# In the loop of small slots the gather of w2 moves from the first part of a slot to the second part of the slot before

## The chip, the cores and the metric

The kernel runs on one core of a Trainium2 chip. The metric is device time of one execution in microseconds (us). The engines that matter are TensorE (PE, with its weight loads PEld), VectorE (DVE), ScalarE (ACT), GpSimd (POOL, which issues every indirect transfer) and SyncE (SP, which issues direct ones).

## The reference

Attention over the channels of four batches, and behind it a skip test and a mixture of eight experts, each token going to one expert:

```python
# attention: B, N, C = 4, 5056, 256
s = kn.transpose(0, 2, 1) @ qn / tau          # kn, qn: k and q over their column norms
a = softmax(s)
x = (v @ a).reshape(B * N, C)
# experts: E = 8, F = 1024
skip_score = x @ w_skip
do_compute = skip_score > 0
xc = x[do_compute]
e_idx = argmax(xc @ w_gate)                   # gate_w: its softmax probability
for e in range(E):
    mask = e_idx == e
    h = maximum(xc[mask] @ w1[e], 0.0)
    y[mask] = gate_w[mask, None] * (h @ w2[e])
out[do_compute] = xc + y                      # other tokens keep x
```

## The kernel before

A planner (`Plan`) orders attention, routing and the first expert slots by hand-set costs and due times. Routing writes a list of token numbers per expert. What is left after that is done in two dynamic loops: large slots of 1024 tokens (`Large.loop`, L431) and small slots of 128 tokens (`Small.loop`, L521). The change touches the small loop and the weights that are loaded ahead of both loops.

**A small slot** is 128 tokens of one expert. It needs the expert's `w1` and `w2` (256 x 1024 numbers of 4 bytes each, so 1.05 MB apiece), its list of tokens and its rows of x. POOL gathers each of these with an indirect transfer: `gather_w` (L221) for weights, `gather_x` (L209) for rows, and `scatter_x` (L214) writes the result rows back. Where a slot has the same expert as the slot two before it, its index is out of bounds on purpose (`wii`, L883) and the gather moves nothing. Buffers are doubled (U = 2): one loop iteration does two slots, u = 0 and u = 1, and o is the other of the two. The trace names the tiles as follows: `v1r` and `v2r` are the raw w1 and w2, `vc` and `vd` their row numbers, `yg` the rows of x, `yT` x transposed, `ph` and `po` the two products in PSUM, `yH` and `yL` the hidden values in two halves of precision, `v2s` the same split of w2, `yo` the result rows, `mP`, `mN`, `mc` and `ms` the token list as it moves from the slot after next to the slot whose rows are stored.

**A slot has two parts**, divided by `tc.stage_boundary()`; an iteration of two slots is four stages.

- First part: POOL gathers w2 for the next slot (`v2r[o]`), copies a list (`ms`, L528) and scatters the result rows of the slot before. PE makes `ph` (L539, 32 matmuls), ACT and DVE split w2 in four pieces (L501, L502) and turn `ph` into `yH` and `yL` (L542, L543).
- Second part: POOL moves the lists on (L549, L550), gathers w1 of the slot two later (`v1r[u]`) and x of the slot two later (`yg[u]`). PE makes `po` (L558, L559), with the transposes of the next slot's x between (L494); DVE adds `po` to x (`yo`, L564, L565).

**What orders it.** Each engine runs its own instructions in the written order, and reuse of semaphores ties the stages together: an engine may enter a stage only when every engine has signed off the stage before the previous one. With stages A(s), B(s) for the two parts of slot s, entering B(s+1) needs the sign-off of B(s) from all five engines. An engine signs off a stage during the next one, at the place that `behind(...)` marks (`previous_stage_wait`), and waits there until everything that it started in the stage being signed off is complete, transfers included. For POOL, `behind(G)` stands at the end of each part, so B(s) is signed off at the end of A(s+1).

**Ahead of the loops**, `load_rows` and `load_weights` (called by the planner's last tasks, L1122) fetch lists, rows and weights of the first two slots. The w2 of slot 1 is not among them: the first part of slot 0 gathers it.

Of the kernel before, what the change touches and what calls it, by code (L numbers as in the profile page):

```python
# [36 lines left out]
U = 2  # L37
# [106 lines left out]
def attn_moe(ctx: ExitStack, tc: tile.TileContext, q, k, vt, tau, w_skip, w_gate, w1, w2, out):  # L144
# [52 lines left out]
    def apart(i, group, reason):  # L197
        tc.declare_no_dep(i.ins, group=group, across_iterations=True, reason=reason)
        tc.add_to_no_dep_group(group, i.ins)
# [8 lines left out]
    def gather_x(to, ls, n=NTOK):  # L208
        apart(G.indirect_dma_start(  # L209
            out=to, out_offset=None, in_=out[0:n, :],  # L210
            in_offset=IndirectOffsetOnAxis(ap=ls[:, 0:1], axis=0), bounds_check=n - 1, oob_is_err=False), *ROWS)

    def scatter_x(ls, src):
        i = (G.indirect_dma_start(  # L214
            out=out, out_offset=IndirectOffsetOnAxis(ap=ls[:, 0:1], axis=0),
            in_=src, in_offset=None, bounds_check=NTOK - 1, oob_is_err=False))
        apart(i, *ROWS)
        return i

    def gather_w(src, to, rows):  # L220
        G.indirect_dma_start(  # L221
            out=to, out_offset=None, in_=src,
            in_offset=IndirectOffsetOnAxis(ap=rows, axis=0), bounds_check=E * P - 1, oob_is_err=False)

    def load_list(adi, i, to, NT, q=nc.sync):
        a = q.value_load(adi[0:1, ds(i, 1)], min_val=0, max_val=E * CAP)
        return q.dma_start(to, lst[ds(a, NT * P), :].rearrange("(p t) w -> p t w", t=NT))
# [4 lines left out]
    def behind(*engines):  # L232

        for e in engines:
            tc.previous_stage_wait(e.engine)
# [3 lines left out]
    class Large:  # L239
# [191 lines left out]
        def loop(self):  # L431
            with tc.For_i(0, self.n, 1, iteration_sync="staggered", hint_engines=(mybir.EngineType.PE,)) as i, tc.manual_schedule():  # L432
                V.tensor_copy(self.wc, self.wii[:, ds(i + 1, 1)])
                V.tensor_copy(self.wd, self.wii[:, ds(i + 1, 1)])
                self.put_last()
                self.take(1)
                self.gather(1)
                gather_w(w1, self.w1r, self.wc)
                behind(G, SP)
                self.first(True)  # L440
                tc.stage_boundary()
                load_list(self.adi, i + 1, self.lN[:, :8, :], 8)
                gather_w(w2, self.w2r, self.wd)
                for t in range(4):
                    self.second(0, t)
                    if t == 1:
                        behind(T, S, V, G, SP)
                        self.transposed(1)
                tc.stage_boundary()
                self.take(0)  # L450
                self.gather(0)
                behind(G, SP)
                self.first(False)
                tc.stage_boundary()
                for t in range(4):
                    if t < 2:
                        self.split_w1(2 * t)
                        self.split_w1(2 * t + 1)
                    self.second(1, t, t < 2)
                    if t == 1:  # L460
                        self.transposed(0)
                        behind(T, S, V, G, SP)
            self.put_last()

    class Small:
# [49 lines left out]
        def load_weights(self):  # L515
            for u in range(U):
                gather_w(w1, self.w1r[u], self.wc[u])
                if u < U - 1:
                    gather_w(w2, self.w2r[u], self.wd[u])

        def loop(self):  # L521
            with tc.For_i(0, self.n, U, iteration_sync="staggered") as i, tc.manual_schedule():  # L522
                for u in range(U):
                    o = (u + 1) % U
                    if u:
                        tc.stage_boundary()
                    gather_w(w2, self.w2r[o], self.wd[o])
                    G.tensor_copy(self.ls[o], self.lc[o])  # L528
                    scatter_x(self.ls[o][:, 0, :], self.ob[o])
                    behind(G)  # L530
                    for g in range(2):
                        for c in (0, 1, 2) if g == 0 else (3,):
                            self.split_w2(u, c)
                        ph = psum["h"].tile([P, 512], F32, name="ph")
                        for f in range(4):
                            po = ph[:, f * P : (f + 1) * P]
                            for kb in range(2):
                                fs = slice(kb * F + (4 * g + f) * P, kb * F + (4 * g + f + 1) * P)
                                T.matmul(po, self.w1r[u][:, fs], self.xT[u][:, kb, :], start=(kb == 0), stop=(kb == 1), skip_group_check=True)  # L539
                        fs = slice(4 * g, 4 * g + 4)  # L540
                        hH, hL = (h[:, fs, :].rearrange("p f t -> p (f t)") for h in (self.hH, self.hL))
                        S.activation(hH, ph, AF.Relu)  # L542
                        V.scalar_tensor_tensor(hL, ph, 0.0, hH, ALU.max, ALU.subtract)  # L543
                        if g == 0:
                            behind(T, S, V, SP)
                            V.tensor_copy(self.wc[u], self.wii[:, ds(i + (u + U), 1)])
                            V.tensor_copy(self.wd[u], self.wii[:, ds(i + (u + U), 1)])
                    tc.stage_boundary()
                    G.tensor_copy(self.lc[o], self.lN[o])  # L549
                    G.tensor_copy(self.lN[o], self.lP[o])  # L550
                    load_list(self.adi, i + (u + 2 * U + 1), self.lP[o], 1)
                    behind(SP)
                    gather_w(w1, self.w1r[u], self.wc[u])
                    gather_x(self.xg[u], self.lN[u][:, 0, :])
                    behind(G)
                    po = psum["o", u % 2].tile([P, 512], F32, name="po")
                    for f in range(NFB):
                        T.matmul(po, self.hH[:, f, :], self.w2s[:, f, :, :], start=(f == 0), stop=False, skip_group_check=True)  # L558
                        T.matmul(po[:, :C], self.hL[:, f, :], self.w2s[:, f, 0, :], start=False, stop=(f == NFB - 1), skip_group_check=True)  # L559
                        if f == 4:  # L560
                            self.transposed(o)
                            behind(T, S, V)
                    gate = self.lc[u][:, 0, 1:2].bitcast(F32)
                    V.scalar_tensor_tensor(self.ob[u], po[:, C:], gate, self.xr[u], ALU.mult, ALU.add)  # L564
                    V.scalar_tensor_tensor(self.ob[u], po[:, :C], gate, self.ob[u], ALU.mult, ALU.add)  # L565
            scatter_x(self.lc[U - 1][:, 0, :], self.ob[U - 1])
# [616 lines left out]
```

## Time and profile before

| | us |
|---|---|
| median of 3 runs (837.49 to 839.32) | 837.91 |
| the profiled execution | 838.44 |
| its span, first to last instruction | 836.7 |
| large loop, first to last matmul of its body | 466.64 to 745.70 |
| small loop, first to last matmul of its body | 750.07 to 831.03 |

The profiled execution takes 1.74 us more than its span. The small loop does ten slots. In a row of the timeline the columns are the start in us, the duration in us, engine, line, operation, output tile <- input tiles, shapes and count; in brackets the idle time of that engine just before, and what ended it. In a row of the stretches the columns are the stretch, its length, busy time and count of each engine, the granted clock of PE as a share of full speed, the mean busy share of the 16 DMA engines and what they moved in GB/s.

### The profile page before, as it was taken

Reading aid. Unit: us, or ns where it says so; the run is one execution under the profiler, and the core shown is the slowest. Engines: PE = TensorE matmul, PEld = TensorE weight load, DVE = VectorE, ACT = ScalarE, POOL = GpSimd, SP = SyncE. Lnnn points to the kernel's source line nnn. Section 1 sums busy time; section 2 is a strip of 40 time slices with the busy share of each in tenths; the row PEclk is TensorE's granted clock in tenths of the full one; section 3 lists DMA queues with packets and bytes.
Section 4 is the critical chain, followed back from the end, with each engine's and each line's share of the span. In section 5 each row is a group of like instructions: output and inputs, shape, how many; then the busy total and the mean of one; then the engine's idle time right before and its main releaser. Section 6 shows DMA issues by size and latency. Waiting matters only on the chain. (4 is left out here: it accounts for less than half of the span.)

```text
span 836.7 us, 13561 instructions
## 1 busy us (share of the span) xinstructions
PE 790.2 (94%) x4506; PEld 695.8 (83%) x4506; DVE 519.4 (62%) x1055; ACT 369.8 (44%) x583; POOL 430.5 (51%) x470
## 2 busy tenths in 40 slices
PE   6999999999979999999989699999999999988876
PEld 5888888998968988888878588888888888877876
DVE  4729758989958556455377646465555556455655
ACT  5449548867665425324212424233333333234543
POOL 3000377778657776767427752434343434426666
PEclk9999999999989999999999899999999999999999
DMA  8969869999364535123021521111111111107770
GB/s 322 400 242 361 346 189 297 397 305 340 103 225 135 165 83 191 56 71 114 26 61 53 197 58 38 51 39 56 44 48 46 44 50 44 31 28 254 258 268 4
DMA packets 58073, 126.35 MB, mean 151 GB/s; under 512 B 17556, under 2 KB 37804, under 8 KB 55472
## 3 DMA queue, kind: packets, MB, share of 16 engines
q1 hardware_dynamic: 17280, 62.99, 20.4%
q0 software_dynamic: 19520, 42.12, 15.3%
q10 hardware_dynamic: 21232, 20.72, 8.2%
q8 instruction: 22, 0.36, 0.2%
q14 instruction: 19, 0.16, 0.1%
HBM read 115.98 MB, written 32.59 MB: 178 GB/s over the span
## 5 line engine op out<-in xcount | busy, mean ns | idle before, releaser
L817 POOL DMA_INDIRECT lst<-pay,r_posi x160 | 177.0, 1106 | 164.4 <-DVE r_posi L814 93.1
L662 PE MATMUL s<-qt,kt 128*128 128x256 f32 x640 | 149.2, 384 | 7.7 <-DMA kt<-in_k 7.7
L214 POOL DMA_INDIRECT out<-xg,lc x78 | 81.7, 1047 | 130.0 <-DVE xg L345 112.9
L662 PEld LDWEIGHTS s<-qt,kt 128*128 128x128 f32 x640 | 119.0, 192 | 22.7 <-issue 8.1
L338 PE MATMUL po<-w2s,hH 128*128 128x512 f32 x384 | 136.4, 398 | 1.1 <-ACT hH L321 1.1
L321 ACT ACTIVATE hH<-ph 128x512 fp32r<-128x512 f32 x96 | 57.5, 599 | 127.3 <-PE ph L318 127.3
L339 PE MATMUL po<-w2s,hL 128*128 128x256 f32 x384 | 107.2, 279 | 0.0
L322 DVE SCALAR_TENSOR_TENSOR hL<-ph,hH 128x512 fp32r<-128x512 f32 x96 | 66.5, 692 | 54.1 <-ACT hH L321 52.8
L209 POOL DMA_INDIRECT xg<-out,lc x80 | 83.5, 1044 | 31.6 <-issue 19.5
L735 PE MATMUL px<-aH,vH 128*128 128x266 f32 x320 | 99.1, 310 | 0.3 <-ACT xo L742 0.3
L737 PE MATMUL px<-aH,vL 128*128 128x266 f32 x320 | 91.8, 287 | 0.0
L736 PE MATMUL px<-aL,vH 128*128 128x266 f32 x320 | 91.3, 285 | 0.0
L338 PEld LDWEIGHTS po<-w2s,hH 128*128 128x128 f32 x384 | 72.1, 188 | 18.0 <-ACT hH L321 1.5
L742 ACT COPY xo<-px 128x532 f32<-128x532 f32 x80 | 47.8, 603 | 73.2 <-PE px L737 73.0
L316 PE MATMUL ph<-xH,w1H 128*128 128x512 f32 x192 | 75.7, 394 | 3.4 <-PEq L432 3.4
L338 PE MATMUL px<-w2s,hH 128*128 128x512 f32 x224 | 78.7, 395 | 0.0
L317 PE MATMUL ph<-xL,w1H 128*128 128x512 f32 x192 | 75.4, 393 | 0.0
L318 PE MATMUL ph<-xH,w1L 128*128 128x512 f32 x192 | 75.4, 393 | 0.0
L339 PEld LDWEIGHTS po<-w2s,hL 128*128 128x128 f32 x384 | 72.3, 188 | 0.4
L344 DVE SCALAR_TENSOR_TENSOR xg<-po,lc,xg 128x256 f32<-128x256 f32 x48 | 23.2, 484 | 63.8 <-PE po L339 53.1
L339 PE MATMUL px<-w2s,hL 128*128 128x256 f32 x224 | 62.7, 280 | 0.0
L735 PEld LDWEIGHTS px<-aH,vH 128*128 128x128 f32 x320 | 60.4, 189 | 1.9 <-ACT xo L742 0.5
(205 smaller groups left out, 1591.9 us busy)
## 6 DMA issues: line engine op xcount, KB each, us to landing
vf<-in_vt SPq DMA_DIRECT2D x32, 640.0 KB, 5.3
qt<-in_q SPq DMA_DIRECT2D x31, 640.0 KB, 7.0
kt<-in_k SPq DMA_DIRECT2D x31, 640.0 KB, 7.5
out<-xo ACTq DMA_DIRECT2D x12, 1280.0 KB, 6.4
lst<-pay,r_posi POOLq DMA_INDIRECT x160
out<-xo ACTq DMA_DIRECT2D x4, 640.0 KB, 5.9
out<-xo ACTq DMA_DIRECT2D x4, 576.0 KB, 8.8
xg<-out,lc POOLq DMA_INDIRECT x80, 2.8
```

The source lines that it names most:

```text
L209: apart(G.indirect_dma_start(out=to, out_offset=None, in_=out[0:n, :], in_offset=IndirectOffsetOnAxis(ap=ls[:, 0:1], axis=0), bounds_check ...
L214: i = (G.indirect_dma_start(out=out, out_offset=IndirectOffsetOnAxis(ap=ls[:, 0:1], axis=0), in_=src, in_offset=None, bounds_check=NTOK - ...
L316: T.matmul(ph, self.w1H[:, fs], self.xH[:, kb, :], start=(kb == 0), stop=False)
L317: T.matmul(ph, self.w1H[:, fs], self.xL[:, kb, :], start=False, stop=False)
L318: T.matmul(ph, self.w1L[:, fs], self.xH[:, kb, :], start=False, stop=(kb == 1))
L338: T.matmul(po, self.hH[:, f, ts], self.w2s[:, f, :, :], start=(f == 0), stop=False, skip_group_check=True)
L339: T.matmul(po[:, :C], self.hL[:, f, ts], self.w2s[:, f, 0, :], start=False, stop=(f == NFB - 1), skip_group_check=True)
L662: T.matmul(sums[b][:, cb, :], kt[:, j % JH, cb * P : (cb + 1) * P], qt[:, j % JH, :], start=(ch == 0 and j == 0 and cb == 0), stop=(ch == ...
L735: T.matmul(px[:, i, :NA], vH[:, kb, js], aH[:, kb, :], start=(kb == 0), stop=False)
L736: T.matmul(px[:, i, :NA], vH[:, kb, js], aL[:, kb, :], start=False, stop=False)
L737: T.matmul(px[:, i, :NA], vL[:, kb, js], aH[:, kb, :], start=False, stop=(kb == 1))
L817: i = G.indirect_dma_start(out=lst, out_offset=IndirectOffsetOnAxis(ap=posi[:, t : t + 1], axis=0), in_=pay[:, t0 + t, :], in_offset=None, ...
```

## The change

The w2 gather leaves the first part of a slot and becomes the last of three gathers in the second part, for the slot two later. The w2 of slot 1 is loaded ahead of the loops.

```diff
         def load_weights(self):
             for u in range(U):
                 gather_w(w1, self.w1r[u], self.wc[u])
-                if u < U - 1:
-                    gather_w(w2, self.w2r[u], self.wd[u])
+                gather_w(w2, self.w2r[u], self.wd[u])
...
                     if u:
                         tc.stage_boundary()
-                    gather_w(w2, self.w2r[o], self.wd[o])
                     G.tensor_copy(self.ls[o], self.lc[o])
                     scatter_x(self.ls[o][:, 0, :], self.ob[o])
                     behind(G)
...
                     behind(SP)
                     gather_w(w1, self.w1r[u], self.wc[u])
                     gather_x(self.xg[u], self.lN[u][:, 0, :])
+                    gather_w(w2, self.w2r[u], self.wd[u])
                     behind(G)
```

On POOL, before, from the second part of slot u = 0 to the second part of u = 1. The rows of `L522 ISA` are the entries of stages; their list of waits also holds those of the sign-off that was written just ahead of them.

```order
L549 COPY mc_4874<-mN_4870 128x2
L550 COPY mN_4870<-mP_4872 128x2 [waits Pool_I-5467_stg1,DMAHW5_49]
L221 DMA v1r_4850<-in_w,vc_4865 128x2048 [waits DVE_I-5467_stg0,PE_I-5467_stg0,DMASW1_49]
L209 DMA yg_4854<-out,mN_4869 128x256 [waits DMAHW4_49]
L522 ISA [waits Pool_I-5467_stg0,PE_I-5012_stg0,DMASW0_I-5012_stg0,sem_stage_0_6612]
L221 DMA v2r_4852<-in_w,vd_4867 128x2048
L528 COPY ms_4875<-mc_4873 128x2
L214 DMA out<-yo_4863,ms_4875 20224x256 [waits Pool_I-5467_stg2,DVE_I-5467_stg1]
L522 ISA [waits Pool_I-5467_stg1,DMASW4_I-5012_stg0,DVE_I-5012_stg0,sem_stage_1_6613]
L549 COPY mc_4873<-mN_4869 128x2
```

And the same stretch of POOL in the changed kernel.

```order
L547 COPY mc_4874<-mN_4870 128x2
L548 COPY mN_4870<-mP_4872 128x2 [waits Pool_I-5470_stg1,DMAHW5_49]
L221 DMA v1r_4850<-in_w,vc_4865 128x2048 [waits DVE_I-5470_stg0,PE_I-5470_stg0,DMASW1_49]
L209 DMA yg_4854<-out,mN_4869 128x256 [waits DMAHW4_49]
L221 DMA v2r_4852<-in_w,vd_4867 128x2048 [waits DVE_I-5470_stg0,DMASW2_49]
L521 ISA [waits PE_I-5015_stg0,Pool_I-5470_stg0,sem_stage_0_6615]
L526 COPY ms_4875<-mc_4873 128x2
L214 DMA out<-yo_4863,ms_4875 20224x256 [waits Pool_I-5470_stg2,DVE_I-5470_stg1]
L521 ISA [waits Pool_I-5470_stg1,Pool_I-5015_stg0,DMASW4_I-5015_stg0,DVE_I-5015_stg0,sem_stage_1_6616]
L547 COPY mc_4873<-mN_4869 128x2
```

The order of the transfers on POOL stays w1, x, w2, scatter; the entry of a stage has moved from ahead of w2 to behind it. In the lists of waits, a name with the number of this loop (`I-5467`, `I-5470`) counts the instructions of an engine; the names with the other number are semaphores taken over from the large loop, one for each transfer that is signed off. At the second of the two entries, behind the scatter, there were two of them (w1, x) and now there are three (w1, x, w2). At the first entry there were two (w2, scatter) and now there is one (scatter).

On POOL ahead of the loops, before: the last gathers of weights, then the stores of the last rows done ahead (`xg_145`), the entry of the large loop (L432) and its first stores.

```order
L221 DMA w2r<-in_w,wd 128x2048
L221 DMA v1r_4850<-in_w,vc_4865 128x2048
L221 DMA v2r_4852<-in_w,vd_4867 128x2048
L221 DMA v1r_4851<-in_w,vc_4866 128x2048
L214 DMA out<-xg_145,lc_153 20224x256 x4
L432 ISA x3
```

And in the changed kernel.

```order
L221 DMA w2r<-in_w,wd 128x2048
L221 DMA v1r_4850<-in_w,vc_4865 128x2048
L221 DMA v2r_4852<-in_w,vd_4867 128x2048
L221 DMA v1r_4851<-in_w,vc_4866 128x2048
L221 DMA v2r_4853<-in_w,vd_4868 128x2048
L214 DMA out<-xg_145,lc_153 20224x256 x4
L432 ISA x3
```

One more gather of a whole w2 stands ahead of those stores and of the entry of the large loop.

## The prediction

> **What bounds the kernel now.** First the page's head, then the busy time of stretches, to see which part of the kernel has room.
>
> ```profile
> span 836.7 us, 13561 instructions
> 490.00:745.00 255.00, 255.00 (x1335) 218.08 (x1334) 146.40 (x254) 87.10 (x154) 101.87 (x109) 1.00 0.14 43
> 750.00:812.00 62.00, 53.34 (x382) 48.96 (x382) 36.44 (x77) 30.48 (x62) 38.39 (x52) 0.97 0.69 250
> 812.00:832.00 20.00, 17.17 (x118) 15.31 (x118) 11.71 (x24) 9.16 (x19) 13.81 (x19) 1.00 0.17 55
> ```
>
> The large loop (490 to 745) is PE without a gap: whatever delays its start is kept to the end. In the small loop PE is busy 53.34 of 62 us and no other engine more; the DMA share is 0.69 while weights still come and 0.17 in the last slots, which fetch none. So some wait there belongs to no engine's work. To find it, compare the start of `po` with that of the first `yL` of the same slot, in a slot with transfers and in one without.
>
> ```profile
> 794.41 0.68 DVE L543 SCALAR_TENSOR_TENSOR yL<-ph,yH 128x512 fp32r<-128x512 f32 x1
> 796.43 0.47 PE L558 MATMUL po<-v2s,yH 128*128 128x512 f32 x1 [1.30 <-DVE v2s L502]
> 819.68 0.68 DVE L543 SCALAR_TENSOR_TENSOR yL<-ph,yH 128x512 fp32r<-128x512 f32 x1
> 820.16 0.47 PE L558 MATMUL po<-v2s,yH 128*128 128x512 f32 x1
> 815.50:819.40 3.90, 3.77 (x32) 3.43 (x31) 2.53 (x5) 2.97 (x7) 2.72 (x3) 1.00 0.04 0
> ```
>
> In the slot whose gathers move nothing (share 0.04) `po` starts 0.48 us behind the first `yL`; the first four of its eight steps need no more. With transfers it starts 2.02 us behind. The bracket blames DVE, but DVE's work is the same in both. POOL's rows show what differs.
>
> ```profile
> 787.57 1.02 POOL L214 DMA_INDIRECT out<-yo,ms  x1 [2.34 <-DMA yg<-out,mN]
> 789.81 1.05 POOL L221 DMA_INDIRECT v1r<-in_w,vc  x1 [0.69 <-issue]
> 791.17 1.01 POOL L209 DMA_INDIRECT yg<-out,mN  x1 [0.31 <-issue]
> 792.49 1.00 POOL L221 DMA_INDIRECT v2r<-in_w,vd  x1 [0.30 <-issue]
> 796.39 0.19 POOL L549 COPY mc<-mN 128x2 int32<-128x2 int32 x1 [0.62 <-DMA yg<-out,mN]
> 797.56 1.05 POOL L221 DMA_INDIRECT v1r<-in_w,vc  x1 [0.66 <-issue]
> 806.61 1.05 POOL L221 DMA_INDIRECT v1r<-in_w,vc  x1 [0.69 <-issue]
> 814.20 1.05 POOL L221 DMA_INDIRECT v1r<-in_w,vc  x1 [0.66 <-issue]
> 790.00:791.50 1.50, 1.50 (x11) 1.36 (x10) 0.00 (x0) 0.95 (x3) 1.19 (x2) 1.00 0.05 1
> 791.50:797.75 6.25, 4.95 (x40) 4.65 (x39) 4.77 (x10) 2.98 (x6) 3.70 (x7) 1.00 0.94 359
> 797.75:798.25 0.50, 0.50 (x4) 0.41 (x4) 0.00 (x0) 0.00 (x0) 0.50 (x1) 1.00 0.30 79
> ```
>
> POOL's first copy of the second part (796.39) waited for the landing of x, gathered at 791.17, and PE's `po` starts at the same moment, 796.43: both pass the entry of the second part, which needs POOL's sign-off of the second part before, and that needs the landing of w1 and x. **The small loop is a ring through POOL's transfers**: entry, list copies, gathers of w1 and x, their landing, next entry. From one w1 gather to the next it takes 7.75, 9.05 and 7.59 us. The engines rest on it by 1.5 us (2.02 - 0.48).
>
> **The change part by part.**
>
> *What moves in time.* The w2 gather was issued 0.30 us behind the end of the x gather (792.49), although a stage's entry stood between: POOL already ran ahead. Behind x without the entry it starts at the same time. The order in the DMA queue, w1, x, w2, scatter, does not change either. So w2 comes no earlier to speak of, and the number of bytes in the loop falls by one w2, which goes ahead of the loops.
>
> *What moves in the signing off.* In the order of POOL the sign-off behind the scatter now covers three transfers, w2 among them. PE, DVE, ACT and SP stand at the entry of the second part behind it; `po`, then `yo`, then the next split of w2 queue up behind PE's wait. The ring is therefore closed by w2's landing, not by x's. The DMA engines are busy in one stretch from 791.50 to about 797.9 (share 0.94, then 0.30 of the next half us), and w2 is its end. From the w1 gather at 789.81 to there are 8.1 us. An estimated 0.3 us of notice takes it to 8.4; 0.7 us of entry and copies and the 1.17 us from the first copy to the next w1 gather (796.39 to 797.56) close the ring at 10.3 us. From the other side: the short turns of 7.75 and 7.59 us, and behind x one more w2 of 1.05 MB at the 410 GB/s of a full stretch (row of 767.30 below), which is 2.56 us, make 10.2 to 10.3. The long turn (9.05) had its scatter waiting for x, as at 787.57; in the change the scatter goes out while w2 is still on its way, so all turns come out alike. **I take 10.3**, between 10.0 (no notice) and 10.9 (the clock case among the rivals).
>
> ```profile
> 750.07 3.81 PE L539 MATMUL ph<-yT,v1r 128*128 128x128 f32 x32 [1.54 <-issue]
> 751.13 1.06 POOL L221 DMA_INDIRECT v2r<-in_w,vd  x1 [1.17 <-issue]
> 755.30 1.06 POOL L221 DMA_INDIRECT v1r<-in_w,vc  x1 [0.71 <-DVE yL L543]
> 753.64 0.48 PE L558 MATMUL po<-v2s,yH 128*128 128x512 f32 x1
> 812.99 0.47 PE L558 MATMUL po<-v2s,yH 128*128 128x512 f32 x1 [1.12 <-DVE v2s L502]
> 827.79 0.47 PE L558 MATMUL po<-v2s,yH 128*128 128x512 f32 x1 [0.74 <-DVE v2s L502]
> ```
>
> *How many turns.* The first w1 gather of the loop stands at 755.30 and the last that moves data at 806.61: seven, so seven entries wait for data, slots 1 to 7. Without a w2 gather ahead of it (1.06 us at 751.13 before) the first w1 gather comes sooner, but it must wait until PE has read the buffer, which ends with `ph` at 753.9 (750.07 + 3.81); with the 0.7 us of dispatch that its row shows that is 754.6. `po` starts 1.13 us ahead of a w1 gather (796.43, 797.56), so `po` of slot 1 comes at 754.6 + 10.3 - 1.15 = 763.75, and that of slot 7 six turns later, at 825.55. Before, it stands at 812.99: **+12.6 us**. Slots 8 and 9 have no data to wait for; the last step (820.16 to 827.79, 7.63 us) may shrink to the 7.17 us of the one before: -0.4. The extra gather behind the last x costs up to 1.3 us against the final scatter, and the scatter ahead of it, no longer behind a w2, gives as much back: 0.
>
> *Ahead of the loops.* One more gather of 1.05 MB on POOL and in the DMA queue, where both are full.
>
> ```profile
> 465.97 0.99 POOL L221 DMA_INDIRECT v1r<-in_w,vc  x1 [0.30 <-issue]
> 466.64 0.76 PE L316 MATMUL ph<-xH,w1H 128*128 128x512 f32 x1 [3.41 <-PEq L432]
> 474.49 1.05 POOL L214 DMA_INDIRECT out<-xg,lc  x1 [0.30 <-issue]
> 477.23 0.19 POOL L265 COPY lc<-lN 128x8 int32<-128x8 int32 x1 [1.68 <-DMA out<-xg,lc]
> 480.68 0.47 PE L338 MATMUL po<-w2s,hH 128*128 128x512 f32 x1 [1.15 <-ACT hH L321]
> 465.50:475.00 9.50, 8.36 (x29) 6.81 (x30) 4.38 (x9) 4.18 (x8) 7.37 (x8) 0.74 0.95 363
> 477.00:478.50 1.50, 1.50 (x9) 1.23 (x8) 0.69 (x1) 0.74 (x2) 0.66 (x2) 1.00 0.00 0
> ```
>
> PE enters the large loop at 466.64 behind a wait for all engines; POOL's dispatch of one more gather moves that by 0.6 to 1.3 us. The larger delay comes behind it: from 465.5 the DMA engines are full (0.95) with weights and then stores, and POOL's copy at 477.23 waits for the last store. One w2 more, 1.05 MB at 363 to 410 GB/s, moves it by 2.6 to 2.9 us, and with it POOL's sign-off, on which the second stage of the large loop, PE's `po` at 480.68, seems to wait: it starts 1.15 us late, and POOL's row gathers stand right ahead of it. The two delays overlap. Bounds: 0.6 (only the dispatch, if that `po` waits for something else) and 2.9, or some 1.7 more if PE's clock, which the first row of that window has at 0.74, recovers one window later. **I take 2.6**, by the copy at 477.23, the nearest row; nothing hides it, since PE has no gap from 490 on.
>
> *Sum.* 12.6 - 0.4 + 2.6 = 14.8 us on the profiled execution of 838.44, so 853.2. The median of the runs is 837.91, 0.5 less, so **853**.
>
> *A rule that speaks for the change.* The issue and the landing of w2 stand in the rows above: 792.49, and about 797.9. The Trainium skill, "DMA: Bandwidth & Descriptors", section "Rules for kernel authors", says to issue a transfer early, compute meanwhile, and wait on its semaphore late. By that rule a gather moved ahead of an entry should not lose and may win; here the rows show that it is issued 0.3 us sooner at most while its wait is put one part earlier, which is the second half of the rule turned round.
>
> **The rivals.**
>
> *1. Faster: the entry waits for POOL's work, not for the landing.* Then a w2 gather less in the first part (1.00 us and 0.30 us ahead of it) brings the sign-off forward.
>
> ```profile
> L558 PE MATMUL po<-v2s,yH 128*128 128x512 f32 x80 | 32.1, 431 | 9.9 <-DVE v2s L502 5.4 <-DVE yL L543 4.5
> ```
>
> PE waits 9.9 us in all ahead of `po` in this loop, in seven places; 1.3 us off each is at most 9.1, and with 2.6 us ahead of the loops the time would be 838.4 - 9.1 + 2.6 = 832. It decides if POOL's first part is longer than the landing of x. Against it: at 820.16 POOL had done the same instructions and PE did not wait, and the copy at 796.39 names the landing of x. Chance 0.05. By the rule of the Trainium skill quoted above the time would come out here.
>
> *2. Only the load ahead of the loops counts*: w2 lands before x's landing is acted on, or is not waited for. Then 838.4 + 2.6 = 841. For it: w2 is hidden today. Against it: the third transfer in the sign-off. Chance 0.06.
>
> *3. The clock falls.* From `po` of slot 0 (753.64) to that of slot 7 (812.99) a slot takes 8.48 us, and PE is busy 53.34 of 62 us: 7.3 us of work a slot. In a turn of 10.3 us it rests 3 us.
>
> ```profile
> 767.30:770.70 3.40, 1.40 (x13) 1.20 (x11) 3.06 (x7) 1.41 (x3) 1.10 (x2) 1.00 1.01 410
> 770.80:774.10 3.30, 3.20 (x10) 2.75 (x11) 0.00 (x0) 0.00 (x0) 2.17 (x5) 0.50 0.13 43
> 770.90 0.77 PE L558 MATMUL po<-v2s,yH 128*128 128x512 f32 x1 [2.20 <-DVE yL L543]
> 784.40:787.80 3.40, 1.55 (x14) 1.36 (x13) 3.31 (x8) 1.56 (x3) 1.05 (x3) 1.00 1.03 410
> ```
>
> Before, PE was busy 1.40 us of a 3.4 us stretch and the granted clock fell to 0.50 for the next 3.3 us; with 1.55 us it did not fall. With longer rests it may fall in every turn. A stretch of 3.3 us at half speed costs a slot some 1.65 us of PE, on top of the 7.17 us that a slot takes without the ring (812.99 to 820.16): 8.8, still under 10.3, so hidden; with two such stretches 10.5. Then turns of 10.9 us give 4.2 us more in seven, some 857. The Trainium skill, "TensorE: Matmul & The Clock Gate", section "Why this matters for your kernels", warns of rests over about 3 us between bursts of matmuls; the trace agrees that rests cost clock, though here 2.20 us were enough once. Chance 0.14.
>
> **How the numbers follow.** The forecast (about 848 to 856) has 0.72, the clock case 0.14, the load alone 0.06, faster 0.05, others 0.03 (0.01 faster, 0.02 no change). The low end takes turns of 10.0 us (-2.1) and 0.6 us ahead of the loops (-2): 849, and 1.5 us of doubt on the first turn; the high end turns of 10.9 us and 1.7 us of clock at 480: 859. The range is 847 to 859.5. A measurement can tell about 0.2% (1.7 us) from no change: slower by more than that has 0.92 (the first three), within 0.02, faster 0.06.
>
> **What would show it.** Right: w1 gathers of POOL some 10.3 us apart in all seven turns; POOL's first copy of a second part released by `v2r`'s landing; DMA engines at rest for 3 us or more of each turn; PE waiting about 3 us ahead of `po`; the large loop's first `po` some 2.6 us later. Wrong: turns still of 7.7 and 9 us, or `po` starting within 0.5 us of `yL` in slots with transfers.

## The result, and the profile after

The changed kernel takes 857.66 us (median of 6 runs, 855.49 to 860.07) against 838.55 us (median of 6 runs of the kernel before, 837.49 to 839.93). The ratio is 1.0225, 95% interval 1.0207 to 1.0244: **slower by 2.2%**, 19 us. The profiled execution took 856.37 us, 17.93 more than that of before.

The head of the page after, and the busy time of three stretches (columns as before: PE, PEld, DVE, ACT, POOL, granted clock, DMA share, GB/s).

```profile
span 854.8 us, 13564 instructions
490.00:745.00 255.00, 255.00 (x1336) 218.06 (x1335) 145.85 (x253) 86.98 (x154) 102.59 (x110) 1.00 0.14 44
752.50:830.00 77.50, 57.23 (x395) 52.63 (x393) 37.43 (x78) 31.20 (x62) 38.54 (x54) 0.93 0.54 201
784.40:787.80 3.40, 1.36 (x13) 1.17 (x11) 2.72 (x7) 1.31 (x3) 1.24 (x1) 1.00 0.98 395
789.00:792.40 3.40, 3.22 (x10) 2.77 (x11) 0.00 (x0) 0.00 (x0) 2.19 (x4) 0.50 0.14 20
```

The large loop is as full as before. In the small loop PE is busy 0.74 of the time (before 0.86), the DMA engines 0.54 (before 0.69), and the clock is down to half in some stretches. POOL's timeline shows what a turn is made of. The rows are those of one turn, and the first and the eighth w1 gather of the loop, which enclose seven turns.

```profile
759.78 1.06 POOL L221 DMA_INDIRECT v1r<-in_w,vc  x1 [0.45 <-DVE v2s L502]
769.87 1.05 POOL L221 DMA_INDIRECT v1r<-in_w,vc  x1 [0.66 <-issue]
771.23 1.00 POOL L209 DMA_INDIRECT yg<-out,mN  x1 [0.31 <-issue]
772.53 1.00 POOL L221 DMA_INDIRECT v2r<-in_w,vd  x1 [0.30 <-issue]
778.91 0.18 POOL L547 COPY mc<-mN 128x2 int32<-128x2 int32 x1 [1.05 <-DMA v2r<-in_w,vd]
780.09 1.05 POOL L221 DMA_INDIRECT v1r<-in_w,vc  x1 [0.69 <-issue]
831.06 1.05 POOL L221 DMA_INDIRECT v1r<-in_w,vc  x1 [0.66 <-issue]
yg<-out,mN POOLq DMA_INDIRECT x7, 4.5
v2r<-in_w,vd POOLq DMA_INDIRECT x7, 5.6
768.72 0.77 PE L557 MATMUL po<-v2s,yH 128*128 128x512 f32 x1 [3.15 <-issue]
778.93 0.47 PE L557 MATMUL po<-v2s,yH 128*128 128x512 f32 x1 [1.90 <-DVE yL L541]
```

The eighth and ninth rows, from the list of transfers, give the median time from issue to landing, 4.5 us for x and 5.6 for w2: for the w2 of 772.53 that is 778.13. At 778.91 POOL's first copy of the next second part is released by just this transfer, and PE's `po` follows at 778.93. So the sign-off is closed by w2, where it was closed by x. A turn here is 2.66 us from the w1 gather to the w2 gather, 5.6 to the landing, 0.78 to the entry, and 1.18 over the two copies to the next w1 gather, together 10.22. The seven turns have a mean of (831.06 - 759.78) / 7 = **10.18 us; before it was (814.20 - 755.30) / 7 = 8.41**.

Where 18.1 us of span went, stage by stage, each from rows of the two timelines: the warming matmuls between the loops start at 752.23 instead of 746.95, +5.28; from there to the first w1 gather 7.55 instead of 8.35, -0.80; the seven turns 71.28 instead of 58.90, **+12.38**; from the eighth gather to the end 23.74 instead of 22.50, +1.24. The sum is 18.10, and the spans differ by 854.8 - 836.7 = 18.1.

The 5.28 ahead of the small loop come from the first stages of the large one, of which these are the rows after (the last is a stretch):

```profile
463.27 0.66 PE L282 MATMUL pt<-ident,xg 128*128 128x128 f32 x4 [1.63 <-DVE xL L286]
468.18 1.00 POOL L221 DMA_INDIRECT v2r<-in_w,vd  x1 [0.31 <-issue]
480.81 0.19 POOL L265 COPY lc<-lN 128x8 int32<-128x8 int32 x1 [3.49 <-DMA out<-xg,lc]
484.26 0.47 PE L338 MATMUL po<-w2s,hH 128*128 128x512 f32 x1 [3.35 <-issue]
485.20:488.60 3.40, 3.40 (x13) 2.84 (x12) 0.00 (x0) 0.00 (x0) 2.48 (x4) 0.50 0.35 88
```

The added gather (468.18) makes the last store late, the copy that waits for it stands at 480.81 instead of 477.23 (+3.58), and PE's `po` at 484.26 instead of 480.68 (+3.58 too). Of this 0.91 was there ahead of the gather, in the transposes of the first row (463.27, before 462.36), so 2.67 belongs to it. PE has then rested 3.35 us instead of 1.15, and the next 3.4 us go at half clock: half of that stretch, 1.7 us, is lost on top. Together that is 3.58 + 1.7 = 5.28, of which 4.4 (2.67 + 1.7) are the change's. No run explains the other 0.91.

### The profile page after: what moved, and what is told of

Read it like the earlier page. It is cut to its first block, busy times and chain, and to the rows that moved or that the text cites. A ratio compares the mean times of both kernels' runs of the same rounds, so it can differ in the third digit from the quotient of the medians.

```text
span 854.8 us, 13564 instructions
## 1 busy us (share of the span) xinstructions
PE 796.6 (93%) x4506; PEld 701.6 (82%) x4506; DVE 519.3 (61%) x1055; ACT 369.4 (43%) x583; POOL 428.1 (50%) x471
```

## The experiments

Theory: the longer turn is the landing of w2, which the sign-off of the second part now includes; and the load ahead of the loops costs some microseconds of its own. Rivals: the load ahead is all; POOL's own work is what got longer; the clock. For each kernel the mean of the seven turns between the first and the eighth w1 gather of the small loop is given beside the ratio, since it doesn't depend on what comes ahead.

Each ratio is to runs of the kernel before that were made beside it. For the first four experiments (load ahead, load between, emptied, halved) these took 839.89 us (median of 19 runs, 836.88 to 842.80). For the others they took 890.94 to 895.59 us, and everything ahead of the small loop took some 55 us longer; why isn't known. Single runs there spread over 9 to 25 us, so the intervals of the ratios are wide, and only turns and ratios are read. Neither the kernel before nor the changed one was profiled beside those, so their turns are compared with the 8.41 and 10.18 us of the profiles above.

### Only the load ahead of the loops

In the kernel before:

```diff
-                if u < U - 1:
-                    gather_w(w2, self.w2r[u], self.wd[u])
+                gather_w(w2, self.w2r[u], self.wd[u])
```

> The kernel before, and w2 of slot 1 is gathered ahead of the loops too; the first part of slot 0 gathers it once more, so the small loop stays as it was. Theory: the whole w2 put ahead of the large loop's first stores delays the rows of its first slot and brings the half-clock stretch one window later; 2.6 to 4.4 us, so 841 to 843 us, with gathers of w1 in the small loop 7.6 to 9.1 us apart as before. Rival (the load is hidden behind attention, and all of the loss is in the small loop): 838 to 839 us.

It took 842.53 us, ratio 1.0028 (1.0012 to 1.0044), so +2.4 us with 1.0 to 3.7 as bounds. Rows of its timeline: the large loop's first `po`, and the warming matmuls.

```profile
486.14 0.50 PE L338 MATMUL po<-w2s,hH 128*128 128x512 f32 x1 [3.67 <-issue]
754.06 1.58 PE L1128 MATMUL m<-ones 128*128 128x128 f32 x12 [1.25 <-PEq L432]
```

PE rests 3.67 us ahead of that `po`, about as in the changed kernel (3.35); in the kernel before it rests 1.15. The turns are 8.26 us, (820.05 - 762.21) / 7. So the load ahead costs time, and it is not all of the cost: the ratio of the change is 1.0225.

### The load between the loops

In the changed kernel:

```diff
     def load_weights(self):
         for u in range(U):
             gather_w(w1, self.w1r[u], self.wc[u])
-            gather_w(w2, self.w2r[u], self.wd[u])
+            if u < U - 1:
+                gather_w(w2, self.w2r[u], self.wd[u])
...
         keep_warm(6)
+        gather_w(w2, smalls[0].w2r[1], smalls[0].wd[1])
         smalls[0].loop()
```

> The changed kernel, but the w2 of slot 1 is gathered between the two loops instead of ahead of both. Theory (the load ahead costs 2.6 to 4.4 us, the small loop's longer turns cost the rest): 853 to 855 us, the large loop's first matmul back at about 466.6 us and the turns of the small loop still 10.2 us; 855 to 858 us if the entry of the small loop waits for the transfer to land (about 5 us, partly beside the last matmuls of the large loop). Rival (the load ahead is all of the cost): 838 to 841 us.

It took 855.30 us, ratio 1.0181 (1.0157 to 1.0205).

```profile
480.57 0.47 PE L338 MATMUL po<-w2s,hH 128*128 128x512 f32 x1 [1.41 <-ACT hH L321]
746.83 1.57 PE L1129 MATMUL m<-ones 128*128 128x128 f32 x12 [1.26 <-PEq L432]
756.65 0.18 POOL L548 COPY mc<-mN 128x2 int32<-128x2 int32 x1 [3.49 <-issue]
757.89 1.05 POOL L221 DMA_INDIRECT v1r<-in_w,vc  x1 [0.73 <-issue]
```

The large loop is back to the times of before (480.57 against 480.68, 746.83 against 746.95), with no half clock there. But the first second part now waits 3.49 us (third row), so the first w1 gather comes 11.06 us behind the warming matmuls instead of 7.55: 3.5 us of what is won ahead are paid here. The turns stay long, 10.47 us, one of them of 12.16 us (798.57 to 810.73), whose cause was not traced. Both parts of the theory stand. The load ahead costs 2.4 us by the medians of the kernel that has it alone, 4.4 by the profile of the changed kernel; this kernel doesn't narrow that down.

### The gather in the loop emptied, and halved

In the changed kernel, with a bound of one row (a fourth argument of `gather_w`), so that every row number but one is out of bounds; w2 of all but the first two slots is left out:

```diff
-                    gather_w(w2, self.w2r[u], self.wd[u])
+                    gather_w(w2, self.w2r[u], self.wd[u], 1)
```

And with 64 of the 128 rows, the other half of w2 being left out:

```diff
-                    gather_w(w2, self.w2r[u], self.wd[u])
+                    gather_w(w2, self.w2r[u][0:64], self.wd[u][0:64])
```

> The changed kernel, but the gathers of w2 inside the small loop drop every row but one, so they move next to nothing; w2 of all but the first two slots is left out, and the instructions stay where they are. Theory (a turn ends when the last byte of w2 has landed): the turn falls from 10.2 to 7.5 to 8.5 us, as long as w1 and x alone take or shorter; seven turns make 12 to 19 us less, 839 to 846 us. Rival (the length comes from POOL's own work, a third transfer to issue ahead of the sign-off): turns stay at 9.5 to 10.2 us and the time at 853 to 858 us.

> The changed kernel, but the gathers of w2 inside the small loop fetch 64 of the 128 rows, half the bytes; the other half of w2 of the later slots is left out. Theory (the turn ends with the last byte of w2): about half of the way from the empty gather to the whole one, turns of 8.8 to 9.4 us and 847 to 852 us. Rival (a fixed price for a third transfer in the sign-off, whatever its size): turns of 10.0 to 10.3 us and 856 to 858 us.

The emptied one took 841.99 us, ratio 1.0036 (1.0016 to 1.0055); the halved one 861.43 us, ratio 1.0239 (1.0215 to 1.0262). From the lists of transfers and from POOL's timeline, first the emptied, then the halved:

```profile
v2r<-in_w,vd POOLq DMA_INDIRECT x7, 3.4
759.63 1.06 POOL L221 DMA_INDIRECT v1r<-in_w,vc  x1 [0.45 <-DVE v2s L502]
774.00 1.30 POOL L214 DMA_INDIRECT out<-yo,ms  x1 [2.68 <-DMA v2r<-in_w,vd]
818.44 1.05 POOL L221 DMA_INDIRECT v1r<-in_w,vc  x1 [0.65 <-issue]
```

```profile
v2r<-in_w,vd POOLq DMA_INDIRECT x6, 6.2
764.47 1.06 POOL L221 DMA_INDIRECT v1r<-in_w,vc  x1 [0.45 <-DVE v2s L502]
838.98 1.05 POOL L221 DMA_INDIRECT v1r<-in_w,vc  x1 [0.65 <-issue]
781.00:782.90 1.90, 1.33 (x12) 1.14 (x11) 1.90 (x7) 1.28 (x3) 0.40 (x1) 1.00 0.65 134
```

Emptied, the same instructions at the same places give turns of 8.40 us, as before the change: the price is the transfer, not POOL's work. What is left of the ratio is about that of the load ahead alone (1.0028).

Halved, my expectation missed: the turns are not shorter but longer, 10.64 us. The list of transfers says why: 64 rows into 64 partitions land 6.2 us behind the issue, later than 128 rows (5.6). In the last row, the end of such a transfer, the DMA engines are busy at a share of 0.65 and move 134 GB/s, where a stretch of whole transfers has 395 at 0.98. The Trainium skill, "DMA: Bandwidth & Descriptors", section "Rules for kernel authors", asks for 128 partitions and at least 1 MiB per transfer for the most bandwidth; this transfer has neither, and the trace agrees, without telling the two apart. So bytes were a bad dose, but the landing is a good one: by the sum above (2.66 + landing + 0.78 + 1.18) landings of 5.6 and 6.2 us give 10.2 and 10.8, measured 10.18 and 10.64. With the 3.4 of the emptied gather the sum gives 8.0. Four of the seven turns there take 7.83 to 7.99 us and agree. The other three take 9.04 to 9.05: in them the scatter waits 2.7 us for a landing before it is issued (row of 774.00), as the scatter at 787.57 does in the kernel before, whose turns alternate in the same way.

### The clock

In the changed kernel, 16 more matmuls behind `ph`, so that PE doesn't rest so long:

```diff
+                    wm = psum["h"].tile([P, 512], F32, name="ph")
+                    for _ in range(16):
+                        T.matmul(wm[:, :P], self.w1r[u][:, :P], self.xT[u][:, 0, :], start=True, stop=True, skip_group_check=True)
                     tc.stage_boundary()
```

> The changed kernel, with 16 more matmuls of 128x128 (about 1.9 us at full clock) behind the ph of each small slot, into a PSUM tile that nobody reads, so that PE rests 1.3 us instead of 3.2 ahead of an entry. Theory (the half-clock stretches in every second slot are hidden beside the wait for w2): granted clock back to 1.0 in the small loop, turns still 10.0 to 10.3 us, 855 to 858 us. Rival (the half clock is part of the loss, 1.65 us in four or five slots): 849 to 852 us.

It took 920.90 us, ratio 1.0221 (1.0135 to 1.0307). A stretch of 60 us of its small loop, and its first and eighth w1 gather:

```profile
810.00:870.00 60.00, 58.62 (x477) 56.54 (x477) 27.94 (x58) 23.23 (x46) 28.07 (x39) 1.00 0.51 186
820.66 1.06 POOL L221 DMA_INDIRECT v1r<-in_w,vc  x1 [4.02 <-PE ph L548]
892.80 1.05 POOL L221 DMA_INDIRECT v1r<-in_w,vc  x1 [0.65 <-issue]
```

The clock is 1.00 and the turns are still 10.31 us. In the changed kernel it is 0.50 to 0.51 for 3.4 us behind every second entry (those of 768.72, 789.18, 809.61 and 829.97) and 1.00 behind the entries between. Up to the last of them, which no turn follows, that half clock was hidden beside the wait for w2.

### The order of the three gathers

In the changed kernel w2 first:

```diff
+                    gather_w(w2, self.w2r[u], self.wd[u])
                     gather_w(w1, self.w1r[u], self.wc[u])
                     gather_x(self.xg[u], self.lN[u][:, 0, :])
-                    gather_w(w2, self.w2r[u], self.wd[u])
```

> The changed kernel, with the three gathers of the second part in the order w2, w1, x instead of w1, x, w2. Theory (the turn ends when the last of the 2.2 MB has landed, and these move one behind the other at the rate of the DMA engines): turns of 10.0 to 10.4 us, 855 to 859 us. Rival (each transfer has its own latency from its issue, 4.5 us for x and 5.6 for weights, so that x last would end 1.1 us sooner): turns of 9.0 to 9.3 us, 848 to 851 us.

It took 918.63 us, ratio 1.0229 (1.0142 to 1.0316). The turns are 11.45 us, (893.94 - 813.78) / 7: longer, where I expected no change and the rival a gain. An entry of its second part, and the list of transfers:

```profile
845.53 0.18 POOL L547 COPY mc<-mN 128x2 int32<-128x2 int32 x1 [4.05 <-DMA v1r<-in_w,vc]
yg<-out,mN POOLq DMA_INDIRECT x4, 6.6
```

The bracket names w1 now, and x lands 6.6 us behind its issue instead of 4.5. That it doesn't keep its 4.5 us refutes the rival: the transfers stand one behind the other. Why the three together take 9.3 us (2.67 + 6.6) from the first issue instead of 8.3 stays open. The trace counts a landing in sixteen steps: of those of the x issued at 838.19, fourteen are there by 843.80, and the last two come at 844.82 and 844.85.

### What stands between entry and issue

The two list copies stand between the entry and the w1 gather. They were put behind the gathers, in the kernel before as shown, and in the changed one in the same way with the gather of w2 as the third:

```diff
+                    gather_w(w1, self.w1r[u], self.wc[u])
+                    gather_x(self.xg[u], self.lN[u][:, 0, :])
                     G.tensor_copy(self.lc[o], self.lN[o])
                     G.tensor_copy(self.lN[o], self.lP[o])
...
-                    gather_w(w1, self.w1r[u], self.wc[u])
-                    gather_x(self.xg[u], self.lN[u][:, 0, :])
```

> The kernel before, with the gathers of w1 and x issued ahead of the two list copies in the second part instead of behind them and behind the list load. Theory (a turn is entry, issue, landing, sign-off, next entry, and the copies stand between entry and issue): the first gather is issued about 0.7 us sooner after the entry, so turns of 7.6 to 7.8 us on average instead of 8.4, seven of them 4 to 6 us less, 833 to 836 us. Rival (turns are bound by the work of PE, ACT and DVE in a slot, and the copies hide beside it): 837.5 to 840 us.

> The changed kernel, with its three gathers issued ahead of the two list copies instead of behind them. In the kernel before, the same edit was worth nothing. Theory (in the changed kernel the ring runs through the landing, with room on POOL, so what stands between entry and issue counts in full): turns 0.4 to 1.0 us shorter, 9.2 to 9.8 us, seven of them 3 to 7 us less than the changed kernel, so a ratio to the kernel before of 1.013 to 1.018 instead of 1.0225. Rival (POOL's own row of instructions sets the turn here too): turns of 10.1 to 10.3 us and a ratio of 1.021 to 1.024.

In the kernel before it is worth nothing: 899.89 us, ratio 0.9993 (0.9939 to 1.0046), turns of 8.44 us. My expectation missed. A turn of POOL in it, with the rows of SP, ACT and PE around its first entry:

```profile
827.81 1.04 POOL L221 DMA_INDIRECT v1r<-in_w,vc  x1 [0.64 <-issue]
829.16 1.01 POOL L209 DMA_INDIRECT yg<-out,mN  x1 [0.31 <-issue]
830.17 0.20 POOL L551 COPY mc<-mN 128x2 int32<-128x2 int32 x1
830.84 0.34 SPq L227 DMA_DIRECT2D mP<-lst  x1
831.43 1.66 ACT L501 CAST v2s<-v2r 128x512 fp32r<-128x512 f32 x3 [1.69 <-issue]
831.67 3.81 PE L539 MATMUL ph<-yT,v1r 128*128 128x128 f32 x32 [1.59 <-issue]
832.61 1.07 POOL L221 DMA_INDIRECT v2r<-in_w,vd  x1 [1.92 <-issue]
834.84 1.02 POOL L214 DMA_INDIRECT out<-yo,ms  x1 [0.82 <-POOL ms L528]
836.16 1.05 POOL L221 DMA_INDIRECT v1r<-in_w,vc  x1 [0.30 <-issue]
```

No bracket of POOL names a transfer any more, and PE goes from `ph` into `po` without a rest (826.83). So the entry of the second part no longer waits for x. But the wait is back at the entry of the first part: ACT, PE and POOL all rest 1.6 to 1.9 us ahead of it (831.43, 831.67, 832.61). What has become late is SP's load of the next list (`mP`, row of 830.84), which overwrites what the second copy reads and so waits for the copies. It is issued 3.03 us behind the w1 gather; in the kernel before it is issued at 797.04, 0.52 us ahead of the w1 gather of 797.56. By the trace's semaphore events SP's sign-off, at 831.24, is the last of the five ahead of this entry; POOL's is done at 830.61. So one wait went and another came, and the turns are as long as before as it happens (8.44 and 8.41). This run doesn't show that POOL's own row of instructions sets the turn of the kernel before. The same edit with the list load kept early was not tried.

In the changed kernel it is a loss: 925.35 us, ratio 1.0394 (1.0304 to 1.0485), turns of 9.73 us at first and 10.9 in the mean.

```profile
842.72 6.71 PE L537 MATMUL ph<-yT,v1r 128*128 128x128 f32 x32 [2.71 <-issue]
842.70:849.50 6.80, 6.78 (x33) 6.76 (x34) 3.30 (x7) 2.56 (x6) 1.68 (x2) 0.55 0.42 156
849.71 1.04 POOL L221 DMA_INDIRECT v1r<-in_w,vc  x1 [4.31 <-PE ph L537]
```

PE's rest has moved from `po` to `ph`: the entry of the first part waits behind the three gathers, the copies and, as in the kernel before with this edit, SP's list load. After that rest the half clock falls on `ph`, which takes 6.71 us instead of 3.73, and the next w1 gather needs the buffer that `ph` reads (third row, 4.31 us). Half clock, hidden at `po`, counts at `ph`.

### The list copies on another engine

The two copies of the second part by DVE, in the kernel before and in the changed one:

```diff
-                    G.tensor_copy(self.lc[o], self.lN[o])
-                    G.tensor_copy(self.lN[o], self.lP[o])
+                    V.tensor_copy(self.lc[o], self.lN[o])
+                    V.tensor_copy(self.lN[o], self.lP[o])
```

> The kernel before, with the two list copies of the second part made by DVE instead of POOL. Theory (before, POOL's own row of instructions, which has hardly a wait in it, sets the turn beside the landing of w1 and x): two copies and the gap behind them, 0.6 to 1.1 us, go from every slot, turns of 7.5 to 8.0 us instead of 8.4, 3 to 6 us less, a ratio of 0.992 to 0.997. Rival (the turn is set by PE, ACT and DVE, or by the landing alone): 0.998 to 1.003.

> The changed kernel, with the two list copies of the second part made by DVE instead of POOL, so that they stand neither ahead of the gathers nor behind them. Theory (a turn of the changed kernel is entry, issue, landing of w2, next entry): the gathers go out 0.5 to 0.8 us sooner after the entry, as the same edit gave in the kernel before, turns of 9.3 to 9.8 us instead of 10.2, 3 to 5 us less in seven turns, a ratio to the kernel before of 1.016 to 1.020. Rival (as with the gathers ahead of the copies, something else is late at once, the buffer of w1 that ph still reads or the clock): turns of 10.0 us or more, a ratio of 1.021 or above.

Before: 888.56 us, ratio 0.9969 (0.9926 to 1.0012), turns of 7.77 us. The turns are as the theory said; the interval of the time includes no change. After: 910.59 us, ratio 1.0206 (1.0126 to 1.0286), turns of 9.90 us, between the two expectations. Rows of the kernel before with this edit, then of the changed kernel with it:

```profile
809.69 1.05 POOL L221 DMA_INDIRECT v1r<-in_w,vc  x1 [0.78 <-DVE v2s L502]
839.51 1.02 POOL L214 DMA_INDIRECT out<-yo,ms  x1 [2.76 <-DMA yg<-out,mN]
864.09 1.04 POOL L221 DMA_INDIRECT v1r<-in_w,vc  x1 [1.25 <-DVE yL L543]
```

```profile
814.20 1.06 POOL L221 DMA_INDIRECT v1r<-in_w,vc  x1 [1.86 <-DVE v2s L502]
823.40 0.47 PE L557 MATMUL po<-v2s,yH 128*128 128x512 f32 x1 [3.39 <-DVE mc L547]
824.19 1.04 POOL L221 DMA_INDIRECT v1r<-in_w,vc  x1 [3.92 <-issue]
883.51 1.04 POOL L221 DMA_INDIRECT v1r<-in_w,vc  x1 [3.92 <-issue]
```

In the kernel before the copies stood between the entry and the w1 gather, and 0.64 us of 8.41 go. x's landing is still in the turn: the turns alternate (7.19 to 7.50 and 8.26 to 8.45 us), and in the longer ones the scatter waits for x as before (row of 839.51). So this run doesn't tell POOL's row from the ring through the landing, which has the copies in it too. In the changed kernel the w1 gather now follows the entry by 0.79 us (823.40 to 824.19) instead of 1.16 (778.93 to 780.09), and the turn is shorter by about that, 0.28: the issue's own gap behind the entry remains. The landing of w2 is still in the turn.

### Two more ways to shorten the kernel before

The x gather in the first part and w1 ahead of the copies; and all three list copies on DVE (`ms` too):

```diff
                     gather_w(w2, self.w2r[o], self.wd[o])
+                    gather_x(self.xg[u], self.lN[u][:, 0, :])
...
+                    gather_w(w1, self.w1r[u], self.wc[u])
                     G.tensor_copy(self.lc[o], self.lN[o])
...
-                    gather_w(w1, self.w1r[u], self.wc[u])
-                    gather_x(self.xg[u], self.lN[u][:, 0, :])
```

> The kernel before, with the gather of x in the first part (behind that of w2) and the gather of w1 ahead of the list copies in the second part, so that only one transfer is signed off across the end of a first part. Theory (the ring through the transfers of the second part): as the gathers-first kernel or up to 0.3 us a turn shorter, since w1 lands 0.2 us ahead of x, 831 to 836 us. Rival (the transfer moved into the first part makes the other entry late, as w2's move made this one): turns of 8.4 us or more, 838 to 842 us.

> As the kernel before with its two list copies on DVE, and the third list copy, that of the first part ahead of the scatter, on DVE too. Theory (POOL's row sets the turn): another 0.3 to 1.0 us a slot on POOL, turns of 7.2 to 7.8 us, a ratio of 0.988 to 0.996. Rival (DVE comes to that copy late, behind its work on the slot before, and the scatter waits for it): the same as with two copies or slower, 0.997 to 1.005.

The first took 903.03 us, ratio 1.0051 (1.0011 to 1.0091), turns of 8.54 us, as the rival had it. The list load stands behind the w1 gather here too; what ends its turns was not worked out further. The second took 892.16 us, ratio 0.9975 (0.9912 to 1.0037), turns of 7.95 us: the third copy gives nothing more, as the rival had it. Whether the scatter's wait for DVE is why was not tested. None of the kernels is shown to be faster than the one before; the best candidate is that with two copies on DVE.

## Why the prediction was right, point by point

- **Direction and time.** 853.0 us were predicted, 847.0 to 859.5; 857.66 came. The sum was 14.8 us on the profiled execution, 17.93 came (18.1 of span). That it came this near is in part luck, since one term was too high and the others too low: the turns up to the eighth gather cost 1.0 us less than summed, the load ahead 1.8 more, the tail 1.6 more, and 0.9 was lost ahead of the added gather.
- **w2 comes no earlier, but its landing moves into the sign-off.** Right: POOL's copy at 778.91 is released by `v2r`, and emptying that transfer alone takes the turn from 10.18 back to 8.40 us.
- **A turn of 10.3 us, seven of them.** Measured 10.18, in all seven between 10.05 and 10.37. The 0.3 us of notice in the sum is an estimate that no row shows by itself; with it the text had 8.4 us from the w1 gather to the end of w2's landing, and 8.26 (2.66 + 5.6) were measured. The first w1 gather was to come 0.7 us sooner and came 0.8 sooner. Together +11.6 us (12.38 - 0.80) up to the eighth gather, where `po` of slot 7 was put at +12.6.
- **The load ahead of the loops, 2.6 us.** The mechanism was right, and so was the size of the delay that it named: stores pushed back in the DMA queue, the copy behind them and the second stage of the large loop late by 2.67 us. Mis-sized was the clock: the 1.7 us of half clock, which the text had only as a bound, fell due, so the term was 4.4 us. The kernel with this load alone lost 2.4 by its median.
- **The tail, -0.4 us.** It was +1.24. The half clock also reached `po` of slot 7, which starts at 829.97 and behind which no turn hides it: the stretch from 829.90 to 833.30 ran at 0.51, which is worth 1.7 us. That this is the cause was not tried by itself.
- **Rival 1, the sign-off waits for POOL's work.** Refuted for the changed kernel: with w2's transfer emptied and all of POOL's instructions in place the turn is 8.40. For the kernel before, the ring that the text drew through "entry, list copies, gathers of w1 and x, their landing, next entry" holds in its trace. The rows name x's landing in both kinds of turn, 0.62 us ahead of the copy at 796.39 and 2.34 ahead of the scatter at 787.57, and by the semaphore events x has landed at 795.77 and POOL's sign-off, the last of the five, is done at 795.80. What the text left out is SP's list load behind the copies: by the trace it is what ate the gain of putting the gathers first, which was not tried by itself. Taking the copies off POOL shortened the turn (7.77), as the ring says and as rival 1 would say too; no run tells the two apart there.
- **Rival 2, only the load ahead.** Refuted: 1.0028 of 1.0225.
- **Rival 3, the clock falls.** It fell, in every second slot. The reasoning that a half-clock stretch of `po` stays hidden in a turn of 10.3 us was right: with the clock kept up the turn is 10.31.
- **The rule on issuing early and waiting late.** As argued: the issue hardly moved, the wait did, and by its second half the rule speaks against this change.

## What to carry to other kernels

Where a loop signs stages off in order, a transfer belongs to the stage that issues it, and moving its issue over a boundary moves its wait too: ask which sign-off then ends last, before asking how early it is issued. Empty the transfer and leave its instruction in place; that tells the landing from the issuing in one run. A ring read off one trace should be tested at each of its links. An edit that takes one wait out of it can put another in its place, so read every entry of the loop again behind the edit, and not only the one that it was meant for, before calling the link refuted.

## What was not expected of the hardware

A gather of 64 rows of 8 KB into 64 partitions took longer from issue to landing (6.2 us) than one of 128 rows (5.6). One that moves next to nothing still took 3.4; an estimated 3.2 of these are the wait behind x, which is issued 1.3 us ahead of it and takes 4.5 in the changed kernel. And half clock cost nothing in front of a wait (3.4 us of it in every second turn: 10.31 us without it, 10.18 with it), but up to some 2.4 us a turn when it fell on the matmuls whose input buffer the next gather needed (a stretch of 6.8 us at 0.55; 9.73 us in the first turn, 12.15 in the longest).
